# Smaller and reordered transfers, casts and hand-overs at the start of a fused attention and MLP kernel

## The chip, the cores and the metric

The kernel runs on one core of one Trainium2 chip. The metric is device time in microseconds (us), as the median of several executions. The median before is 295.24 us (three runs, 294.39 to 295.44).

## The reference

The first stage is a linear ("efficient") attention over 8 batches, 8 heads, 576 positions and 64 dimensions; the second is an MLP with a leaky ReLU on the 4608 resulting tokens.

```python
q_s = softmax(q, axis=-1)                       # over the 64 dimensions
k_s = softmax(k, axis=2)                        # over the 576 positions
kv  = einsum('bhsd,bhse->bhde', k_s, v)
att = einsum('bhsd,bhde->bhse', q_s, kv)
x   = att.transpose(0, 2, 1, 3).reshape(4608, 512)
h   = x @ w_in                                  # 512 x 2048
out = maximum(0.01 * h, h) @ w_out              # 2048 x 512
```

Inputs and output are float32; the kernel's matmuls take bf16.

## The kernel before, in words

The order of all work is written out by hand: every engine executes its instructions in the order in which the program lists them, and semaphores only make it wait. There is no scheduler.

**Layout.** A batch's q, k and v are loaded as `[128 partitions, 4 head pairs' columns, R = 9 rows, 64]` float32 (`load`, L72, on SyncE's queue, SP). Partitions 0 to 63 hold the even half of the heads and 64 to 127 the other half, and position is split into L = 64 partitions by R = 9 rows. `xT` holds the attention's result transposed, `[128 channels, 4 channel blocks, 4608 tokens]`, in bf16. `w_in_sb` and `w_out_sb` hold the weights in bf16; both are loaded on GpSimd's queue (POOL), which casts from float32 in the transfer. A transfer of w_in covers 64 partitions, two blocks and a range of columns, so one range of columns takes four transfers (`load_w_in`, L129).

**Per batch.** k: a maximum over positions (`k_tree`, `k_allmax`; for batch 0 through TensorE, `k_max_pe` and `k_all_pe`), subtraction (`k_sub`, for batch 0 `k_sub_ps`), `k_exp`. v: a cast to bf16 (`v_cast`, L209), on ScalarE for batches 0 and 1 and on GpSimd later. `kv` (for batch 0 `kv_pair`) multiplies ke by v, with a column of ones for the sum; `kd_make` (or `kd_rec`, `kd_one`) divides by it. q: `q_max`, `q_sub`, `q_exp`, `q_sum`, `q_norm`; for the first four rows of batch 0, `q_first` does the first steps on ScalarE. Then q is turned: batch 0 by TensorE (`q_transpose`, then `q_keep` copies PSUM into `qT`), later batches by a DMA transpose (`q_turn` into `qX`). `attend` or `attend_x` multiplies by kd and copies the result into `xT`.

**The MLP.** It works on 9 tiles of 512 tokens. In `layer1` each of 16 column blocks j of w_in takes four matmuls, one for each channel block, in the order 0, 2, 1, 3; `leaky` on ScalarE copies the PSUM result to a `gj` tile. In `layer2` the 16 blocks of gj are multiplied by w_out, for four groups of 128 tokens; `store` copies the result out of PSUM and issues two DMAs on SP.

**The first tile** is special. It has only batch 0's tokens, and it starts before all of q is there: rows 0 to 3 (RA) give its first 256 tokens. Four pairs of column blocks are begun with the channel blocks 0 and 2 (L641 to L645), then `attend(0, [1, 3], ...)` delivers the other two (L646), and the pairs are finished. `wake` keeps TensorE at work with products of zeros while there is nothing else. The rest of q (R1 is rows 4 and 5, R2 rows 6 to 8) and all of batch 1's preparation hang on hooks: `at(t, u, fn)` puts a step behind unit u of tile t. In tile 0 units 0 to 15 are the column blocks of the first 256 tokens, 16 to 31 those of the second 256, and 32 to 47 the blocks of layer 2.

**Loads.** `gate` is a tiny GpSimd copy that makes POOL's queue wait for some of k before weights are issued; `hold_sync` is a tiny DMA that makes SP's queue wait for a part of a weight before further loads are issued. In the kernel before, SP waits for part of w_in's second half (L560) and then issues k, q and v of batch 1; POOL waits for k of batch 1 (L564) and then issues w_out in five parts. PSUM is handed out in buffers of one bank, six in the pool `psB`.

Of the kernel before, what the change touches and what calls it, by code (L numbers as in the profile page):

```python
# [25 lines left out]
def kernel(  # L26
# [89 lines left out]
    xT = xT_pool.tile([P, NB, T], BF16)  # L116

# [11 lines left out]
    def load_w_in(fh):  # L129
        fs = slice(fh * (F // 2), (fh + 1) * (F // 2))  # L130
        for gg in range(2):
            for hp in range(2):
                nc.gpsimd.dma_start(  # L133
                    out=w_in_t[hp * D : (hp + 1) * D, gg, :, fs], in_=w_in_r[gg, hp, :, :, fs]
                )
# [82 lines left out]
    def q_begin(b):  # L218
        st[b]["qe"] = qe_pool.tile([P, R, HL, D], BF16, name="qe")
        if b == 0:  # L220
            st[b]["qT"] = qT_pool.tile([P, NB, R, L], BF16, name="qT", tag="qT")
# [179 lines left out]
    def q_keep(eng, b, r0, n, gs=slice(0, 4)):  # L401
        o, i = st[b]["qT"][:, gs, r0 : r0 + n], st[b]["ps", r0][:, gs]
        if eng is nc.scalar:
            eng.copy(out=o, in_=i)
        else:
            eng.tensor_copy(out=o, in_=i)

    def attend(b, gs, c0, n, eng):

        ps = psB_pool.tile([P, len(gs), n], FP32, name="po", tag=BANK_TAG)  # L410
        for i, g in enumerate(gs):
            nc.tensor.matmul(
                ps[:, i],
                lhsT=kd2[b % 2][:, g],
                rhs=st[b]["qT"][:, g].rearrange("c r l -> c (r l)")[:, c0 : c0 + n],
                start=True,
                stop=True,
            )
        step = gs[-1] - gs[0] if len(gs) == 2 else 1
        o = xT[:, gs[0] : gs[-1] + 1 : step, b * S + c0 : b * S + c0 + n]  # L420
        if eng is nc.scalar:
            eng.copy(out=o, in_=ps)
        else:
            eng.tensor_copy(out=o, in_=ps)  # L424
# [10 lines left out]
    def attend_x(b, g, rs, eng):  # L435
        hh, gg = divmod(g, 2)
        n = (rs.stop - rs.start) * L
        ps = psB_pool.tile([P, n], FP32, name="po", tag=BANK_TAG)
        qX = st[b]["qX"].rearrange("c (r g) (h l) -> c g h r l", g=2, h=2)
        nc.tensor.matmul(  # L440
            ps.rearrange("p (r l) -> p r l", l=L), lhsT=kd2[b % 2][:, g], rhs=qX[:, gg, hh, rs]
        )
        c0 = b * S + rs.start * L
        o = xT[:, g, c0 : c0 + n]
        if eng is nc.scalar:
            eng.copy(out=o, in_=ps)  # L446
        else:
            eng.tensor_copy(out=o, in_=ps)

    def layer1(j, ph, c0, n, part=slice(0, 4), first=True, last=True):  # L450
        for i, cb in list(enumerate((0, 2, 1, 3)))[part]:
# [3 lines left out]
                rhs=xT[:, cb, c0 : c0 + n],  # L455
# [45 lines left out]
    held = const_pool.tile([1, 2, 128], BF16)  # L501

# [7 lines left out]
    load_w_in(0)  # L510
# [20 lines left out]
    v_cast(nc.scalar, 0, 0)  # L531
    v_cast(nc.scalar, 0, 1)
    k_sub_ps(0, 1)
    nc.gpsimd.tensor_copy(out=gate[:, 0:1], in_=st[0]["k"][:, HL - 1, R - 1, D - 1 : D])
    load_w_in(1)
# [10 lines left out]
    q_keep(nc.scalar, 0, 0, 4, slice(0, 4, 2))  # L546
    q_keep(nc.vector, 0, 0, 4, slice(1, 4, 2))
# [15 lines left out]
    st[1]["v"] = load(v, 1, "v_raw", [(ALLH, ALLR)])  # L563
    nc.gpsimd.tensor_copy(out=gate[:, 0:1], in_=st[1]["k"][:, 0, 0, 0:1])  # L564
    for j0, j1 in ((0, 2), (2, 4), (4, 8), (8, 12), (12, 16)):
        load_w_out(slice(j0, j1))

# [3 lines left out]
    at(0, 11, lambda: q_transpose(0, 4, 2), lambda: q_keep(nc.vector, 0, 4, 2))  # L571
    at(0, 13, lambda: q_transpose(0, 6, 3), lambda: q_keep(nc.vector, 0, 6, 3))
    at(0, 15, lambda: attend(0, [0, 2], 256, 256, nc.scalar))
    at(0, 15, lambda: attend(0, [1, 3], 256, 256, nc.vector))
    at(0, 17, lambda: attend(0, [0, 1, 2, 3], 512, 64, nc.scalar))
    at(0, 15, lambda: k_begin(1), lambda: q_begin(1), lambda: k_tree(1, H0), lambda: k_tree(1, H1))
    at(0, 15, lambda: k_allmax(1), lambda: k_sub(nc.gpsimd, 1, H0), lambda: k_sub(nc.vector, 1, H1))
    at(0, 15, lambda: q_max(1, RA), lambda: q_sub(nc.gpsimd, 1, RA))
    at(0, 15, lambda: q_max(1, RB), lambda: q_sub(nc.gpsimd, 1, RB))
    at(0, 29, lambda: k_exp(1, H1))  # L580
    at(0, 31, lambda: k_exp(1, H0), lambda: v_cast(nc.scalar, 1, 0))
    at(0, 33, lambda: q_exp(1, RA), lambda: q_sum(1, RA), lambda: q_norm(1, RA))
    at(0, 33, lambda: v_cast(nc.scalar, 1, 1), lambda: q_exp(1, RB))
    at(0, 38, lambda: kv(1), lambda: q_sum(1, RB), lambda: q_norm(1, RB), lambda: kd_make(1))
    at(0, 41, lambda: q_turn(1, RA))
    at(0, 43, lambda: q_turn(1, RB))
    at(0, 44, lambda: hold_sync(1, w_out_sb[0:1, 11, 0:128]), lambda: load_all(2))
    for i in range(8):
        at(0, 47, lambda i=i: attend_x(1, i % 4, (RA, RB)[i // 4], nc.scalar))


    XR = (slice(0, 5), slice(5, R))
# [53 lines left out]
    attend(0, [1, 3], 0, 256, nc.scalar)  # L646
# [11 lines left out]
    for j in range(NF):  # L658
        for tsub in range(NTS):
            layer2(pout[tsub], g_sb, tsub, j)  # L660
        if j == NF - 1:
            for tsub in range(NTS):
                store(tsub * P, pout[tsub])
        run(0, 32 + j)
# [57 lines left out]
```

## Time and profile before

| | before |
|---|---|
| median of three runs | 295.24 us |
| the profiled execution, its own time | 293.87 us |
| span of its profile | 292.1 us |
| TensorE (PE) busy | 277.7 us, 95% |
| VectorE (DVE) busy | 145.5 us, 50% |
| ScalarE (ACT) busy | 148.5 us, 51% |
| GpSimd (POOL) busy | 86.0 us, 29% |
| granted TensorE clock | 1.0 |

Times within the profile are counted from the start of the span. "PEld" is TensorE's weight load, which runs beside the matmuls. The page cuts the span into 40 slices and gives each engine's busy tenths. The chain of waits follows the work that ended last backwards, from each step to what released it; in a line of it stand the start, the length and the engine with the line of the kernel. A line of a timeline has the start, the length, the engine, the line, the operation, output and input, and in brackets the idle time before it and what ended that. A DMA's landing time is counted from its issue. The bandwidth that is shown counts bytes as written, so a transfer that casts float32 to bf16 reads twice what is counted.

### The profile page before, as it was taken

The page shows a single profiled execution, that of the slowest core. Times are in us where ns is not written, and L with a number is a line of the kernel's source. Part 1 is how long each engine was busy: PE and PEld are TensorE (multiplying, and loading weights), DVE is VectorE, ACT ScalarE, POOL GpSimd, SP SyncE. Part 2 cuts the span into 40 slices and gives each one's busy share as a digit, 9 for nine tenths or more (in the row PEclk, how much of TensorE's full clock was granted, in tenths as well). Part 3 has the DMA queues.
Part 4 walks back from the last instruction along what each step waited for, and adds up shares of the span by engine and source line. Part 5 has one row for each costly group of instructions (what it writes and reads, how often), then busy time and mean ns, then how long its engine had stood idle before and what let it go on. Part 6 is the DMA issues. An engine that isn't in the chain of part 4 may idle for free.

```text
span 292.1 us, 4216 instructions
## 1 busy us (share of the span) xinstructions
PE 277.7 (95%) x1616; PEld 138.1 (47%) x1643; DVE 145.5 (50%) x240; ACT 148.5 (51%) x268; POOL 86.0 (29%) x61
## 2 busy tenths in 40 slices
PE   6696999999999999999999999999999999999995
PEld 2265844444544455454445444544454444444443
DVE  3947957696790696189276546745540200110011
ACT  4956680678068506941684339533953066016400
POOL 4645280008039208703920391029200000000000
PEclk9999999999999999999999999999999999999999
DMA  7999984989939454963298139913141310131032
GB/s 256 311 212 388 249 134 81 346 302 393 210 75 346 158 117 104 359 187 84 70 336 252 38 72 317 283 39 72 38 81 36 74 36 1 36 79 31 0 73 73
DMA packets 38948, 46.35 MB, mean 159 GB/s; under 512 B 18320, under 2 KB 21648, under 8 KB 38928
## 3 DMA queue, kind: packets, MB, share of 16 engines
q1 hardware_dynamic: 35488, 41.75, 48.7%
q0 software_dynamic: 3280, 4.20, 8.2%
q8 instruction: 13, 0.21, 0.3%
q10 hardware_dynamic: 160, 0.13, 0.1%
q14 instruction: 7, 0.06, 0.1%
HBM read 36.70 MB, written 9.44 MB: 158 GB/s over the span
## 4 chain that ended last, share of the span: by engine, by line
PE 84%; DMA 5%; POOL 3%; DVE 2%; ACT 2%; issue 2%; SPq 0%; POOLq 0%; ACTq 0%
PE pout L473 40%; PE ph L452 39%; DMA w_in_sb<-in_moe_w_in_dram 3%; PE pkv L295 3%; PE po L440 2%; DMA k_raw<-in_k_dram 2%; POOL w_in_sb L133 1%; POOL k_raw L195 1%; DVE t L162 1%; ACT xT L446 1%; ACT vb L213 1%; ACT qe L264 0%; SPq L79 0%; DVE xT L424 0%; DVE m L179 0%
## 5 line engine op out<-in xcount | busy, mean ns | idle before, releaser
L452 PE MATMUL ph<-xT,w_in_sb 128*128 128x512 bf16 (+1 forms) x625 | 126.9, 357 | 4.5 <-DMA w_in_sb<-in_moe_w_in_dram 1.9
L473 PE MATMUL pout<-w_out_sb,gj 128*128 128x512 bf16 (+2 forms) x581 | 128.7, 373 | 0.8 <-issue 0.5
L461 ACT ACTIVATE gj<-ph 128x512 bf16<-128x512 f32 x144 | 82.5, 603 | 58.5 <-PE ph L452 57.9
L452 PEld LDWEIGHTS <-w_in_sb 128*128 128x128 bf16 x640 | 62.1, 98 | 66.2 <-issue 5.4
L473 PEld LDWEIGHTS <-gj 128*128 128x128 bf16 x592 | 57.0, 98 | 62.5
L467 DVE COPY out_sb<-pout 128x512 f32<-128x512 f32 (+1 forms) x34 | 22.7, 675 | 88.2 <-PE pout L473 82.0
L195 POOL TENSOR_TENSOR k_raw<-k_raw,kall 128x2304 f32<-128x2304 f32 (+1 forms) x6 | 29.1, 4842 | 83.6 <-DVE kall L187 69.3
L446 ACT CAST xT<-po 128x256 bf16<-128x256 f32 (+1 forms) x56 | 19.3, 407 | 47.5 <-PE po L440 47.5
L273 DVE TENSOR_REDUCE qsum<-qe 128x36 f32<-128x2304 bf16 (+4 forms) x11 | 19.8, 1799 | 37.8 <-ACT qe L264 37.8
L256 POOL TENSOR_TENSOR q_raw<-q_raw,qmax 128x2304 f32<-128x2304 f32 (+4 forms) x11 | 31.1, 2836 | 25.2 <-DVE qmax L226 25.2
L203 ACT ACTIVATE ke<-k_raw 128x2304 bf16<-128x2304 f32 (+2 forms) x11 | 17.6, 1596 | 10.6 <-POOL k_raw L195 9.4
L280 DVE TENSOR_TENSOR qe<-qe,qrec 128x2304 bf16<-128x2304 bf16 (+4 forms) x12 | 21.7, 1810 | 0.4
L226 DVE TENSOR_REDUCE qmax<-q_raw 128x36 f32<-128x2304 f32 (+4 forms) x11 | 19.4, 1789 | 0.0
L264 ACT ACTIVATE qe<-q_raw 128x2304 bf16<-128x2304 f32 (+4 forms) x11 | 16.9, 1533 | 0.0
L215 POOL CAST vb<-v_raw 128x1152 bf16<-128x1152 f32 x12 | 13.4, 1148 | 0.0
L440 PE MATMUL po<-qX,kd 128*128 128x256 bf16 (+1 forms) x56 | 11.5, 286 | 0.2
L162 DVE TENSOR_TENSOR t<-k_raw 128x1024 f32<-128x1024 f32 (+1 forms) x10 | 10.1, 1011 | 3.1 <-DMA k_raw<-in_k_dram 2.9
L324 PE MATMUL pout<-zero 128*128 128x512 bf16 x26 | 8.8, 466 | 1.4 <-POOL zero L101 1.3
L467 ACT COPY out_sb<-pout 128x512 f32<-128x512 f32 (+1 forms) x3 | 1.6, 549 | 16.5 <-PE pout L473 16.5
L162 DVE TENSOR_TENSOR t<-t 128x256 f32<-128x256 f32 (+2 forms) x20 | 9.6, 478 | 0.7
L295 PEld LDWEIGHTS <-ke 64*128 64x128 bf16 x252 | 7.2, 93 | 3.2 <-ACT gj L461 1.7
L295 PE MATMUL pkv<-vb,ke 64*128 64x129 bf16 x252 | 8.5, 216 | 0.1
(55 smaller groups left out, 94.0 us busy)
## 6 DMA issues: line engine op xcount, KB each, us to landing
out_dram<-out_sb SPq DMA_DIRECT2D x70, 128.0 KB, 2.4
q_raw<-in_q_dram SPq DMA_DIRECT2D x7, 1152.0 KB, 8.7
v_raw<-in_v_dram SPq DMA_DIRECT2D x7, 1152.0 KB, 11.7
k_raw<-in_k_dram SPq DMA_DIRECT2D x6, 1152.0 KB, 5.8
k_raw<-in_k_dram SPq DMA_DIRECT2D x4, 576.0 KB, 5.7
w_in_sb<-in_moe_w_in_dram POOLq DMA_DIRECT2D x8, 256.0 KB, 6.8
w_out_sb<-in_moe_w_out_dram POOLq DMA_DIRECT2D x3, 512.0 KB, 12.0
v_raw<-in_v_dram SPq DMA_DIRECT2D x2, 576.0 KB, 7.3
```

The lines of the kernel that those rows point to most:

```text
L162: nc.vector.tensor_tensor(out=o, in0=i0, in1=i1, op=ALU.max)
L195: eng.tensor_tensor(out=ks, in0=ks, in1=st[b]["kall"][:, hs].unsqueeze(2).to_broadcast([P, n, R, D]), op=ALU.subtract,)
L226: nc.vector.tensor_reduce(out=m, in_=st[b]["q"][:, :, rs], axis=AX.X, op=ALU.max)
L256: eng.tensor_tensor(out=qs, in0=qs, in1=st[b]["qmax", rs.start].unsqueeze(3).to_broadcast([P, HL, n, D]), op=ALU.subtract,)
L273: nc.vector.reduce_sum(out=qsum, in_=st[b]["qe"][:, rs], axis=AX.X)
L280: nc.vector.tensor_tensor(out=qes, in0=qes, in1=st[b]["qrec", rs.start].unsqueeze(3).to_broadcast([P, n, HL, D]), op=ALU.mult,)
L295: nc.tensor.matmul(pkv[hh][:, gg, 0:129], lhsT=st[b]["ke"][rows, r, 2 * gg : 2 * gg + 2].rearrange("p h d -> p (h d)"), rhs=vb2[b % 2][row ...
L446: eng.copy(out=o, in_=ps)
L452: nc.tensor.matmul(ph, lhsT=w_in_sb[:, cb, j * P : (j + 1) * P], rhs=xT[:, cb, c0 : c0 + n], start=(i == 0 and first), stop=(i == NB - 1 a ...
L461: nc.scalar.activation(out=o, in_=ph, func=AF.Prelu, alpha=LEAKY_SLOPE)
L467: copy(out=out_sb, in_=pout)
L473: nc.tensor.matmul(pout, lhsT=g_sb[j // 2][:, j % 2, tsub * P : (tsub + 1) * P], rhs=w_out_sb[:, j, os], start=(j == 0), stop=(j == NF - 1),)
```

## The change

It has five parts.

1. `load_w_in` takes a range of column blocks. The first half of w_in is loaded as before; the second half is issued as two quarters of four transfers each, behind a gate that reads head pair 1 of k and not head pair 3.
2. The first half of batch 0's v is cast by GpSimd, between w_in's first half and the gate.
3. The channel blocks of `xT` are stored in the order 0, 2, 1, 3 (`XB`), and `qT` has a dimension for the head pair, so that blocks 0 and 2 lie side by side. Head groups [0, 2] and [1, 3] are then contiguous. In the first tile, `attend(0, [1, 3], ...)` is listed after the second of the four begun pairs and not after the fourth. The hooks of batch 0's remaining q move from units 11, 13, 15 to 9, 12, 14.
4. Batch 1: q is split into rows 0 to 4 and 5 to 8 (`XR`); its maximum and subtraction go first, the subtraction of k is done by VectorE alone, and the order of ScalarE's work is q_exp, both k_exp, both v casts, q_exp. `kv` moves from unit 38 to 40. Of its eight `attend_x`, the sixth and the eighth are evacuated by VectorE, and the eight stand ahead of the first tile's stores.
5. Batch 1's v is issued on SP's queue only once the first part of w_out has landed; `load_all(2)` follows the second `q_turn` directly.

The diff, in its core:

```diff
@@ w_in @@
-    def load_w_in(fh):
-        fs = slice(fh * (F // 2), (fh + 1) * (F // 2))
+    def load_w_in(j0, j1):
+        fs = slice(j0 * P, j1 * P)
...
-    load_w_in(0)
+    load_w_in(0, 8)
+    v_cast(nc.gpsimd, 0, 0)
     k_begin(0)
...
     k_exp(0, slice(1, 2))
-    v_cast(nc.scalar, 0, 0)
     v_cast(nc.scalar, 0, 1)
+    nc.gpsimd.tensor_copy(out=gate[:, 0:1], in_=st[0]["k"][:, 1, R - 1, D - 1 : D])
+    load_w_in(8, 12)
+    load_w_in(12, 16)
     k_sub_ps(0, 1)
-    nc.gpsimd.tensor_copy(out=gate[:, 0:1], in_=st[0]["k"][:, HL - 1, R - 1, D - 1 : D])
-    load_w_in(1)
     k_exp(0, H1)
@@ layouts @@
+    XB = (0, 2, 1, 3)
...
-            st[b]["qT"] = qT_pool.tile([P, NB, R, L], BF16, name="qT", tag="qT")
+            st[b]["qT"] = qT_pool.tile([P, 2, 2, R, L], BF16, name="qT", tag="qT")
...
-    def q_keep(eng, b, r0, n, gs=slice(0, 4)):
-        o, i = st[b]["qT"][:, gs, r0 : r0 + n], st[b]["ps", r0][:, gs]
+    def q_keep(eng, b, r0, n, ggs=slice(0, 2)):
+        o = st[b]["qT"][:, ggs, :, r0 : r0 + n].rearrange("p g h r l -> p g h (r l)")
+        i = st[b]["ps", r0].rearrange("p (h g) r l -> p g h (r l)", g=2)[:, ggs]
...
-                rhs=st[b]["qT"][:, g].rearrange("c r l -> c (r l)")[:, c0 : c0 + n],
+                rhs=st[b]["qT"][:, g % 2, g // 2].rearrange("c r l -> c (r l)")[:, c0 : c0 + n],
...
-        step = gs[-1] - gs[0] if len(gs) == 2 else 1
-        o = xT[:, gs[0] : gs[-1] + 1 : step, b * S + c0 : b * S + c0 + n]
+        x0 = XB[gs[0]]
+        o = xT[:, x0 : x0 + len(gs), b * S + c0 : b * S + c0 + n]
...
-        o = xT[:, g, c0 : c0 + n]
+        o = xT[:, XB[g], c0 : c0 + n]
...
-                rhs=xT[:, cb, c0 : c0 + n],
+                rhs=xT[:, XB[cb], c0 : c0 + n],
@@ loads of batch 1 @@
     st[1]["q"] = load(q, 1, "q_raw", [(ALLH, ALLR)])
-    st[1]["v"] = load(v, 1, "v_raw", [(ALLH, ALLR)])
     nc.gpsimd.tensor_copy(out=gate[:, 0:1], in_=st[1]["k"][:, 0, 0, 0:1])
     for j0, j1 in ((0, 2), (2, 4), (4, 8), (8, 12), (12, 16)):
         load_w_out(slice(j0, j1))
+    hold_sync(1, w_out_sb[0:1, 1, 0:128])
+    st[1]["v"] = load(v, 1, "v_raw", [(ALLH, ALLR)])
@@ hooks @@
-    at(0, 11, lambda: q_transpose(0, 4, 2), lambda: q_keep(nc.vector, 0, 4, 2))
-    at(0, 13, lambda: q_transpose(0, 6, 3), lambda: q_keep(nc.vector, 0, 6, 3))
-    at(0, 15, lambda: attend(0, [0, 2], 256, 256, nc.scalar))
-    at(0, 15, lambda: attend(0, [1, 3], 256, 256, nc.vector))
-    at(0, 17, lambda: attend(0, [0, 1, 2, 3], 512, 64, nc.scalar))
+    at(0, 9, lambda: q_transpose(0, 4, 2), lambda: q_keep(nc.vector, 0, 4, 2))
+    at(0, 12, lambda: q_transpose(0, 6, 3), lambda: q_keep(nc.vector, 0, 6, 3))
+    at(0, 14, lambda: attend(0, [0, 2], 256, 256, nc.scalar))
+    at(0, 14, lambda: attend(0, [1, 3], 256, 256, nc.vector))
+    at(0, 17, lambda: attend(0, [0, 2, 1, 3], 512, 64, nc.scalar))
     at(0, 15, lambda: k_begin(1), lambda: q_begin(1), lambda: k_tree(1, H0), lambda: k_tree(1, H1))
-    at(0, 15, lambda: k_allmax(1), lambda: k_sub(nc.gpsimd, 1, H0), lambda: k_sub(nc.vector, 1, H1))
-    at(0, 15, lambda: q_max(1, RA), lambda: q_sub(nc.gpsimd, 1, RA))
-    at(0, 15, lambda: q_max(1, RB), lambda: q_sub(nc.gpsimd, 1, RB))
-    at(0, 29, lambda: k_exp(1, H1))
-    at(0, 31, lambda: k_exp(1, H0), lambda: v_cast(nc.scalar, 1, 0))
-    at(0, 33, lambda: q_exp(1, RA), lambda: q_sum(1, RA), lambda: q_norm(1, RA))
-    at(0, 33, lambda: v_cast(nc.scalar, 1, 1), lambda: q_exp(1, RB))
-    at(0, 38, lambda: kv(1), lambda: q_sum(1, RB), lambda: q_norm(1, RB), lambda: kd_make(1))
-    at(0, 41, lambda: q_turn(1, RA))
-    at(0, 43, lambda: q_turn(1, RB))
-    at(0, 44, lambda: hold_sync(1, w_out_sb[0:1, 11, 0:128]), lambda: load_all(2))
+    at(0, 15, lambda: q_max(1, XR[0]), lambda: q_sub(nc.gpsimd, 1, XR[0]), lambda: k_allmax(1))
+    at(0, 15, lambda: k_sub(nc.vector, 1, H0), lambda: k_sub(nc.vector, 1, H1))
+    at(0, 15, lambda: q_max(1, XR[1]), lambda: q_sub(nc.gpsimd, 1, XR[1]))
+    at(0, 32, lambda: q_exp(1, XR[0]), lambda: k_exp(1, H0), lambda: k_exp(1, H1))
+    at(0, 32, lambda: v_cast(nc.scalar, 1, 0), lambda: v_cast(nc.scalar, 1, 1), lambda: q_exp(1, XR[1]))
+    at(0, 32, lambda: q_sum(1, XR[0]), lambda: q_norm(1, XR[0]), lambda: q_turn(1, XR[0]))
+    at(0, 40, lambda: kv(1), lambda: q_sum(1, XR[1]), lambda: q_norm(1, XR[1]), lambda: kd_make(1))
+    at(0, 43, lambda: q_turn(1, XR[1]), lambda: load_all(2))
     for i in range(8):
-        at(0, 47, lambda i=i: attend_x(1, i % 4, (RA, RB)[i // 4], nc.scalar))
+        eng = nc.vector if i in (5, 7) else nc.scalar
+        at(0, 47, lambda i=i, eng=eng: attend_x(1, i % 4, XR[i // 4], eng))
@@ first tile @@
         begun.append(ph)
-    attend(0, [1, 3], 0, 256, nc.scalar)
+        if j == 2:
+            attend(0, [1, 3], 0, 256, nc.scalar)
...
             layer2(pout[tsub], g_sb, tsub, j)
+        run(0, 32 + j)
         if j == NF - 1:
             for tsub in range(NTS):
                 store(tsub * P, pout[tsub])
-        run(0, 32 + j)
```

More of the change, by code (lines that the diff above doesn't have):

```diff
@@ L501 @@
     held = const_pool.tile([1, 2, 128], BF16)
+    XR = (slice(0, 5), slice(5, R))
     def hold_sync(i, src):
@@ L545 @@
         kd_one(nc.vector, 0, 0, hh)
-    q_keep(nc.scalar, 0, 0, 4, slice(0, 4, 2))
-    q_keep(nc.vector, 0, 0, 4, slice(1, 4, 2))
+    q_keep(nc.scalar, 0, 0, 4, slice(0, 1))
+    q_keep(nc.vector, 0, 0, 4, slice(1, 2))
     attend(0, [0, 2], 0, 256, nc.scalar)
@@ L588 @@
     for i in range(8):
-        at(0, 47, lambda i=i: attend_x(1, i % 4, (RA, RB)[i // 4], nc.scalar))
-    XR = (slice(0, 5), slice(5, R))
+        eng = nc.vector if i in (5, 7) else nc.scalar
+        at(0, 47, lambda i=i, eng=eng: attend_x(1, i % 4, XR[i // 4], eng))
     for b in range(3, B):
```

## The prediction

> **What bounds the kernel now.** I read the page first. PE is busy 95% of the span. Its row over 40 slices of 7.3 us:
>
> ```profile
> PE   6696999999999999999999999999999999999995
> ```
>
> The low digits stand in the first four slices; later it is at 9 tenths to the last. So time is won early, and whatever starts the second token tile earlier moves the whole tail. Next I read the chain of waits, in order of time (start us, us, what). Its early pieces:
>
> ```profile
> 7.96 2.50 POOL w_in_sb L133 x4
> 10.46 2.23 issue
> 12.70 0.02 POOLq L256
> 12.71 0.19 POOL gate L534
> 12.90 1.67 POOL w_in_sb L133 x3
> 14.57 9.07 DMA w_in_sb<-in_moe_w_in_dram
> 23.64 0.14 issue
> 23.77 1.69 PE ph L452 x14
> ...
> 51.69 2.20 ACT xT L446 x7
> 53.88 0.04 issue
> 53.93 1.24 PE ph L452 x5
> ```
>
> The reader sees the last of w_in's transfers holding PE until 23.77, and after that the evacuations of batch 1's attention holding the second tile until 53.93. Third, the waits of PE alone, from 14 to 56 us (total, times, longest):
>
> ```profile
> PE ph L452 <- DMA w_in_sb<-in_moe_w_in_dram: 1.9, 1, 1.9
> PE ph L452 <- ACT xT L422: 1.4, 2, 0.7
> ```
>
> The 1.4 are two stops, 19.12 to 19.79 and 28.21 to 28.93 in PE's timeline. Fourth, VectorE's timeline, since a wait that goes lets the next one show. It carries the rest of batch 0's q (rows R1 and R2):
>
> ```profile
> 22.06 0.69 DVE L273 TENSOR_REDUCE qsum<-qe 128x8 f32<-128x512 bf16 x1 [3.54 <-ACT qe L264]
> 22.78 0.20 DVE L275 RECIPROCAL qrec<-qsum 128x8 f32<-128x8 f32 x1
> 23.02 0.69 DVE L280 TENSOR_TENSOR qe<-qe,qrec 128x512 bf16<-128x512 bf16 x1
> 23.63 0.95 DVE L273 TENSOR_REDUCE qsum<-qe 128x12 f32<-128x768 bf16 x1
> 24.61 0.23 DVE L275 RECIPROCAL qrec<-qsum 128x12 f32<-128x12 f32 x1
> 24.87 0.96 DVE L280 TENSOR_TENSOR qe<-qe,qrec 128x768 bf16<-128x768 bf16 x1
> ```
>
> R2's q is normalised at 25.83, R1's at 23.71. PE turns them at 26.39 and 25.30, so this chain ends only 0.5 us ahead of PE.
>
> **Step 1, half of v on GpSimd.** ACT gives up one cast of 1152 elements (two of them take 2.19, so 1.1). On POOL the same shape takes 1137 to 1158 ns in all twelve of its runs. It starts behind the four first w_in issues at 10.46 (that v landed at 2.29 + 6.8 = 9.1) and ends near 11.6; its ke is ready at 12.07, so kv_pair(0,0) starts near 12.1 and not at 13.16. The full 1.06 does not arrive: q_transpose waits for q_norm, which VectorE ends at 14.07, while before it started at 14.66 behind wake(4). So q_transpose, kv_pair(0,1), the copy of qT, attend and its evacuation move by 0.53 to 0.57, and the first layer1 matmul goes from 17.00 to 16.43. Queued behind the cast on POOL are the gate and w_in's second half; the gate now waits for the subtraction ending at 11.36 and not the one at 12.65, so w_in issues from 11.9 rather than 12.83.
>
> **Step 2, head pairs.** q_keep on VectorE still follows ScalarE's (the changed instruction list keeps that wait), so qT's new order is worth nothing. attend([1,3]) goes ahead of two of the four begun pairs: it runs at 17.3 (kd ready at 16.6), is evacuated by 18.2, and PE passes from the begun pairs to their second halves at 18.43 without the 0.67 stop, against 19.79 before. Gain so far 1.36.
>
> **Step 3, w_in in quarters.** It adds four issues at 0.6 us on POOL, and the last four wait for the first half's landings (13.7, 14.8, 16.3, 17.4), so POOL is done at 18.0 instead of 15.2; next in its queue is q_sub of R1, which began at 17.74 and now begins at 18.0. Its reader, q_exp, comes at 20.04, so 0.3 us is hidden by a margin of 1 us. The transfers are bound by bandwidth: DMA share is over 1.0 in every 2 us window from 4 to 40 us, and the three 256 KB parts of the second half landed 1.2 to 1.3 us apart (18.7, 20.0, 21.2). Quarters of 128 KB then land 0.63 apart, the third quarter at 20.0, the fourth at 22.5. The fourth is earlier than 23.64 because batch 1's k, held until part of the last columns is there, now goes out at 21.3 and not at 19.39. PE reaches column block 8 at 18.43 + 16 matmuls x 0.109 = 20.2. The 1.85 stop is gone.
>
> The Trainium skill ("DMA: Bandwidth & Descriptors", Anatomy of one DMA) gives each software DMA about 2 us of fixed cost beside its bytes, and its rules for kernel authors want 1 MiB or more in one, which speaks against quarters. If that cost were paid in series, the four extra DMAs would add 8 us by an estimate from that page. The rows above, 256 KB every 1.25 us with several in flight, do not show it paid in series.
>
> **Step 4, what is late next.** The q chain. q_exp R1 stands behind two leakys on ScalarE and so moves with step 2 by 1.36: R1 is normalised at 22.35, R2 at 24.47. But the transposes were moved up, to units 9 and 12. PE is at unit 9's hook at 21.07 and waits 1.3 us; from 22.35 it turns R1 (0.25), does blocks 10 to 12 (1.3), waits from 23.9 to 24.47, turns R2 (0.5), does 13 and 14 (0.86), four attends (0.5) and 15 (0.43), and stands at 26.75. ScalarE's evacuation (0.58) ends then; VectorE's (0.69) ends at 27.05, 0.1 us late. Before, the second half of the tile could start at 28.93. Gain 2.1: of the 1.85 and 0.72 stops won, some 1.9 comes back as a wait for q.
>
> **Step 5, layer 2.** The second half needs 7.1 us as before, so layer 2 starts at 33.95 and not 36.03. w_out must hold against that. Batch 1's k lands at 25.3 (24.9 before), q at 29.7 (29.4). In the windows from 24 to 30 us 392 to 407 GB/s move, that is the fp32 loads almost alone; from 32 us 202 to 215, w_out alone, counted at half its reads. So w_out gets through when q is done: its first part at about 30.9 (33.3 before, behind v), the second at 32.2, needed at 33.95 and 35.7. v goes out at 31.5. Batch 2's k, as large and alone, took 6.0 us to land, so v lands near 38. Meanwhile w_out's third part (j 4 to 7) is pushed to about 37.6 against a need of 37.4. I take 0.1, with 0 to 0.9 as bounds.
>
> **Step 6, batch 1.** VectorE starts k at 26.95 (28.85 before). Its work grows by one subtraction (1.36) that POOL gave up: 3.6 trees, 1.5 q_max, 2.3 k_allmax, 2.7 subtractions, 1.2 q_max, to 38.3. ScalarE: q_exp 34.4 to 35.7, k_exps to 38.3, v casts (2.3) to 40.6, q_exp to 41.7. kv now stands behind block 8, at 33.95 + 9 x 0.862 = 41.7. It is ready with 1 us to spare. q_turn of the second part follows at 44.4 and lands at 47.8 (3.4 us, as before); attend_x is due at 49.3. Nothing waits there.
>
> **Step 7, attend_x.** ScalarE had eight evacuations in 2.52; now it has six and VectorE two, in parallel. That is worth about 0.3 of the 2.20 in the chain, bounds 0 and 0.65. The four output copies on VectorE now follow them (2.48 us), with batch 2's trees behind, at 53.7 and not 56.07, shifted as much as PE. Batch 2's loads go out some 4 us earlier. So the tail shifts as a whole.
>
> **Sum.** 2.1 + 0.3 - 0.1 (w_out) - 0.1 (rounding of late hand-overs) = 2.2 us. The profiled execution took 293.87 (span 292.1 and 1.8 around it), so it would be 291.7. The median of the runs shown is 295.24, 1.4 above that execution; it becomes 293.0.
>
> **Rivals.** First, the gain is mostly eaten: the early shift of 0.55 fails (VectorE is held up while POOL casts; its norm took 2.12 at 71.10 beside POOL's casts against 1.49 at 46.42), and w_out's third part costs its full 0.9. Against it: the VectorE subtractions beside this cast read PSUM and fp32, and one beside POOL at 34.82 took 1.36 against 1.32. It gives 2.2 - 0.55 - 0.8, so 0.8 us: 294.4.
>
> Second, slower: v, sent behind w_out's first part, is late. Its price begins when v lands later than 39.4, since two casts (2.25) stand between it and kv at 41.7. If v is only served after all the software queue's work, the DMA engines have 2.5 MB of w_out reads and 1.18 MB of v left at 33.6; at 410 GB/s v lands at 42.6 to 42.8. kv then waits 3.4 us, and 2.2 - 3.4 makes it 1.2 slower: 296.4. From a landing at 41.6 on the change loses. For it: v is last in line. Against it: from 28 to 30 us, with w_out issued at 25.8, 392 GB/s still moved, so plain loads went ahead of w_out.
>
> The Trainium skill ("DMA: Bandwidth & Descriptors", Queues, rings and completion order) has the engines take turns between queues by packet. By an estimate from that page v and w_out would share evenly and v land at 39.4, at the edge where it starts to cost. The window just named shows no even turns.
>
> Third, the q chain costs nothing because it starts earlier than I think (ScalarE's first leakys come at once): then PE loses only the evacuation at the half's end, and the second half starts at 25.4 and not 28.93. With step 7 and the 0.2 of losses that is 3.6: 291.6.
>
> **How the numbers follow.** Forecast 0.55, first rival 0.22, second 0.13, third 0.10. A measurement here can tell about 0.5%, 1.5 us, from no change. The forecast case (1.4 to 2.9 us) and the third lie beyond it nearly always: faster 0.64. The first rival and the second at its lower prices: same 0.24. The second with another delay on top: slower 0.12. Range 291.3 to 296.0: the third rival with step 7 at its upper bound, and most of the second rival's way to 296.4.
>
> **What would show it.** Right: the first layer1 matmul near 16.4; no wait of PE for w_in; waits of PE for VectorE's qe before two transposes, some 1.3 and 0.5 us; layer 2 from 34; kv from 41.7 without a wait; the second tile from 51.5. Wrong: a wait of PE for w_out or of ScalarE for v of over 1 us, or layer 2 starting at 35 or later.

## The result, and the profile after

The changed kernel takes 297.34 us (median of nine runs, 296.20 to 299.83), the kernel before 295.19 us in the same comparison. The ratio is 1.0094 with a 95% interval of 1.0071 to 1.0118: slower by 2 to 3 us, where 2.2 us were to be won. The profiled execution took 299.2 us (span 297.4), so it lies 1.9 above its median, while that of before (293.87) lies 1.3 below; of the 5.3 us between the two spans some 3 are the choice of execution. Part of the difference among executions goes with a clock: most executions of before have a mean granted TensorE clock of 0.994 (21 of the 31 of one comparison), the profiled one 1.0; those of the changed kernel have 0.977 to 0.988.

The rows of the page over 40 slices (7.4 us each) show where it differs. First PE, then its granted clock:

```profile
PE   6597996999999999999999999999999999999995
PEclk9779998999999999999999999999999999999999
```

The clock was 9 in every slice before. It is now low in the second and third slice and again in the seventh, and the low busy digit in that slice (6) is new as well. From the ninth slice on the two pages are alike: the second token tile starts at 58.99 instead of 53.27 (there with a stop of 0.28 right behind its first matmuls, here with none), so 5.4 later in effect, and the span is 5.3 longer. So all of it happens in the first 59 us.

The chain of waits of the changed kernel (start us, us, what):

```profile
9.64 0.66 DVE t L163
10.30 0.59 POOL w_in_sb L134
10.89 1.16 POOL vb L216
...
16.64 5.20 DMA w_in_sb<-in_moe_w_in_dram
...
22.53 4.65 DMA k_raw<-in_k_dram
...
28.24 5.46 DMA w_out_sb<-in_moe_w_out_dram
...
34.27 12.05 DMA v_raw<-in_v_dram
...
46.35 2.22 ACT vb L214 x2
...
57.25 1.42 ACT xT L448 x4
```

Before, the chain went over w_in to PE at 23.77. Now it never touches PE before 48.6: it runs from GpSimd's cast (`vb` on POOL) through w_in, batch 1's k, w_out's first part and v to the casts of v, each load issued only when the one before had landed. (Between the cast and the gate it has 1.80 us as "issue"; the gate reads head pair 1 of k, whose subtraction on VectorE ended at 13.72.) The waits of PE from 8 to 62 us (total, times, longest):

```profile
PE kT L331 <- POOL gate L512: 2.3, 1, 2.3
PE pkv L296 <- ACT vb L214: 2.1, 2, 1.7
PE kT L331 <- DVE kmax L163: 2.0, 1, 2.0
PE psum_qt L390 <- ACT gj L463: 1.3, 1, 1.3
PE psum_qt L390 <- DVE qe L281: 0.4, 1, 0.4
```

The waits for w_in (1.9) and for `xT` (1.4) are gone, and the two before q's transposes are there as forecast. (The first of them carries ScalarE's name, but the leaky had long been done; VectorE's norm of R1, ending at 26.13, is what came last.) The first row lies in front of the first k maximum and was 1.7 before. The second and third were not forecast, and the experiments will show them to be the two causes.

**The first, near 11 us.** VectorE's timeline of the changed kernel, at the last steps of k's maximum for the second half:

```profile
9.19 1.69 DVE L163 TENSOR_TENSOR t<-t 128x256 f32<-128x256 f32 x2
10.91 1.28 DVE L163 TENSOR_TENSOR kmax<-t,k_raw 128x128 f32<-128x128 f32 x1
```

POOL's timeline at the same time:

```profile
10.85 1.19 POOL L216 CAST vb<-v_raw 128x1152 bf16<-128x1152 f32 x1
```

The same steps in the kernel before:

```profile
8.76 0.74 DVE L162 TENSOR_TENSOR t<-t 128x256 f32<-128x256 f32 x2
9.54 0.29 DVE L162 TENSOR_TENSOR kmax<-t,k_raw 128x128 f32<-128x128 f32 x1
```

A step of 0.29 us takes 1.28 when it lies beside GpSimd's cast, and the one ahead of it is stretched by 0.95 too. The maximum is ready at 12.19 instead of 9.83 (0.43 of that is a later first load), PE waits 1.95 us for it, and its clock is half from 11.6 to 18.4: kv_pair takes 1.16 instead of 0.68. The first layer1 matmul comes at 20.25, before at 17.00.

**The second, near 46 us.** ScalarE's wait from 8 to 62 us:

```profile
ACT vb L214 <- DMA v_raw<-in_v_dram: 4.3, 1, 4.3
```

v is issued at 34.27 and lands at 46.35. kv starts at 47.55 (42.16 before) after 1.75 us of standstill, waits 0.37 more for the second cast, and then PE has half clock again from 49.1 to 52.5: layer 2's 27 matmuls behind kv take 7.39 us, against 5.99 for the same ones at full clock in the run with v early below.

### The profile page after: what moved, and what is told of

The parts are those of the page before. It is cut to its first block, busy times and chain, and to the rows that moved or that the text cites. A ratio compares the mean times of both kernels' runs of the same rounds, so it can differ in the third digit from the quotient of the medians.

```text
span 297.4 us, 4224 instructions
## 1 busy us (share of the span) xinstructions
PE 281.5 (95%) x1616; PEld 139.7 (47%) x1643; DVE 149.5 (50%) x243; ACT 146.8 (49%) x265; POOL 86.0 (29%) x65
## 2 busy tenths in 40 slices
DMA packets 39524, 46.35 MB, mean 156 GB/s; under 512 B 18384, under 2 KB 22736, under 8 KB 39504
## 4 chain that ended last, share of the span: by engine, by line
PE 81%; DMA 11%; POOL 2%; ACT 2%; issue 2%; DVE 1%; SPq 1%; ACTq 0%; POOLq 0%
PE pout L475 39%; PE ph L454 37%; DMA v_raw<-in_v_dram 4%; DMA k_raw<-in_k_dram 3%; PE pkv L296 3%; PE po L442 2%; DMA w_out_sb<-in_moe_w_out_dram 2%; DMA w_in_sb<-in_moe_w_in_dram 2%; DVE t L163 1%; POOL w_in_sb L134 1%; ACT vb L214 1%; ACT xT L448 1%; POOL vb L216 0%; SPq L507 0%; POOL gate L567 0%
## 5 line engine op out<-in xcount | busy, mean ns | idle before, releaser
L196 POOL TENSOR_TENSOR k_raw<-k_raw,kall 128x2304 f32<-128x2304 f32 x5 | 25.3, 5066 | 77.8 <-DVE kall L188 63.6
L448 ACT CAST xT<-po 128x320 bf16<-128x320 f32 (+1 forms) x54 | 18.8, 405 | 47.7 <-PE po L442 47.7
L204 ACT ACTIVATE ke<-k_raw 128x2304 bf16<-128x2304 f32 (+2 forms) x11 | 17.5, 1596 | 11.7 <-POOL k_raw L196 8.6
L227 DVE TENSOR_REDUCE qmax<-q_raw 128x36 f32<-128x2304 f32 (+4 forms) x11 | 19.5, 1788 | 0.0
L216 POOL CAST vb<-v_raw 128x1152 bf16<-128x1152 f32 x13 | 14.6, 1151 | 0.0
L442 PE MATMUL po<-qX,kd 128*128 128x320 bf16 (+1 forms) x56 | 11.6, 286 | 0.3
L325 PE MATMUL pout<-zero 128*128 128x512 bf16 x26 | 10.0, 513 | 1.5 <-POOL zero L101 1.3
L163 DVE TENSOR_TENSOR t<-t 128x256 f32<-128x256 f32 (+2 forms) x20 | 10.5, 526 | 0.7
## 6 DMA issues: line engine op xcount, KB each, us to landing
v_raw<-in_v_dram SPq DMA_DIRECT2D x7, 1152.0 KB, 11.6
```

The lines of the kernel that those rows point to most:

```text
L163: nc.vector.tensor_tensor(out=o, in0=i0, in1=i1, op=ALU.max)
L196: eng.tensor_tensor(out=ks, in0=ks, in1=st[b]["kall"][:, hs].unsqueeze(2).to_broadcast([P, n, R, D]), op=ALU.subtract,)
L227: nc.vector.tensor_reduce(out=m, in_=st[b]["q"][:, :, rs], axis=AX.X, op=ALU.max)
```

## The experiments

The theory: two parts of the change each cost more than the other three win. GpSimd's cast holds up VectorE's two-input steps in SBUF, and v behind w_out's first part comes too late; both leave PE standing, and the clock then makes it dearer. The rivals: one of the two does it all; the head pairs, quarters and the new order of batch 1 are themselves at fault; or the clock alone is. Ratios below are against the kernel before, run on the same chip beside them, with 95% intervals.

### Undo one part, the other, both

**Cast back on ScalarE** (the changed kernel otherwise):

```diff
     load_w_in(0, 8)
-    v_cast(nc.gpsimd, 0, 0)
...
+    v_cast(nc.scalar, 0, 0)
     v_cast(nc.scalar, 0, 1)
```

> The changed kernel with the first half of batch 0's v cast by ScalarE again, everything else as changed. Theory 1 (the GpSimd cast holds VectorE's k_tree beside it: the second k maximum ended at 12.19 us instead of 9.83, PE then stood still for 2 us and its granted clock fell to 0.5 until 18.8): the k_tree steps of the second half take 0.29 to 0.43 us each again, the clock stays 1.0 from 10 to 20 us, and the first layer1 matmul starts at 17.0 to 17.5 instead of 20.25. Rival (the late prologue comes from slower first loads or from the quarters of w_in): the first layer1 matmul stays near 20. Theory 2 (v of batch 1 is late, it landed at 46.3): that wait stays or grows, kv starts near 45 to 46 and the time falls by only 1 to 2 us, to 295.5 to 296.5.

Measured: 296.36 us, ratio 1.0047 (1.0024 to 1.0070). The two steps of k's maximum take 0.74 and 0.29 again, and the first layer1 matmul comes at 18.60. It is not 17.0, as kv_pair now waits 1.44 us for ScalarE's cast, as it did before, and half clock follows for 3.4 us. v still lands late (44.9), kv waits 1.95 and 0.37. Still slower: the cast is not all of it.

**v ahead of w_out again** (the changed kernel otherwise):

```diff
     st[1]["q"] = load(q, 1, "q_raw", [(ALLH, ALLR)])
+    st[1]["v"] = load(v, 1, "v_raw", [(ALLH, ALLR)])
...
-    hold_sync(1, w_out_sb[0:1, 1, 0:128])
-    st[1]["v"] = load(v, 1, "v_raw", [(ALLH, ALLR)])
```

> The changed kernel with batch 1's v loaded directly behind its q again, ahead of w_out. Theory 2: the wait of ScalarE's v cast (4.3 us) and of PE's kv (1.75 + 0.37 us) goes, and the clock stays 1.0 from 49 to 53 us, where it was 0.5; that is worth 2.4 us of waiting and about 1.7 us of slow clock, some 4 us: 293 to 294. The first layer1 matmul stays near 20.2. Rival (w_out then lands later and PE waits for it instead): PE waits for w_out from 36 to 38 us, and the time stays at 296 to 298.

Measured: 294.80 us, ratio 1.0000 (0.9975 to 1.0025). kv runs at 45.38 without a wait, and from 20 us on the clock is full. The stretched steps and the 1.95 us wait are as in the changed kernel. So v's place makes 0.94% of it, 2.8 us. The time is above the 293 to 294 expected, and level with the kernel before: the cast alone eats about what the other parts win, not more.

**Both undone:**

```diff
-    v_cast(nc.gpsimd, 0, 0)
...
+    v_cast(nc.scalar, 0, 0)
...
+    st[1]["v"] = load(v, 1, "v_raw", [(ALLH, ALLR)])
...
-    hold_sync(1, w_out_sb[0:1, 1, 0:128])
-    st[1]["v"] = load(v, 1, "v_raw", [(ALLH, ALLR)])
```

> Both undone: v's cast on ScalarE, batch 1's v ahead of w_out; w_in in quarters, the head-pair order, the earlier hooks and batch 1's new order stay. If the two theories are all that made the change slower, the steps that are left give the forecast's rest: first layer1 matmul near 17, layer 2 from 34 to 34.5, 2 us faster than before: 293 to 293.5. If there is a third cause (the order of batch 1, w_out's landing), it is 294.5 or more, with a new wait of PE that the profile names.

Measured: 293.48 us, ratio 0.9966 (0.9943 to 0.9989): faster than before by 1.0 us. That is half of the 2 us expected, and layer 2 starts at 36.34 and not at 34 to 34.5, as the first layer1 matmul comes at 18.72, behind a stretch of half clock. Taken together, the head pairs, the quarters and batch 1's order win; that they are at fault as a whole is ruled out, and what each is worth, the quarters apart (below), was not separated. Set on top of this kernel, the cast costs 0.34% (1.0 us, about what the intervals of the two ratios allow as noise; 0.47% where v is late too, 0.53% on the kernel before), v's place 0.81% (2.4 us; 0.94% with the cast), and the two together 1.28%, 3.8 us.

### Each of the two alone, on the kernel before

**Only the cast:**

```diff
     load_w_in(0)
+    v_cast(nc.gpsimd, 0, 0)
...
-    v_cast(nc.scalar, 0, 0)
```

> The kernel before with one edit: the first half of batch 0's v cast by GpSimd behind w_in's first half, as in the change. Theory 1 (the cast holds VectorE's operations that read two SBUF inputs, whatever else was changed): the two t steps and the k maximum of the second head pairs take about 3 us instead of 1.03, the second k maximum ends near 12 instead of 9.83, the clock falls to 0.5 for two stretches (run mean 0.988 and not 0.994 to 1.0), and the first layer1 matmul comes near 19.5 to 20. Since PE later waits less for w_in, the time is 1 to 2.5 us above before. Rival (the cast does harm only with the quarters and the moved gate): the k maximum ends near 9.9 and the time is within 0.5 us of before or below.

Measured: 296.13 us, ratio 1.0053 (1.0030 to 1.0075). VectorE's and POOL's timelines of this run:

```profile
8.78 1.68 DVE L162 TENSOR_TENSOR t<-t 128x256 f32<-128x256 f32 x2
10.49 1.29 DVE L162 TENSOR_TENSOR kmax<-t,k_raw 128x128 f32<-128x128 f32 x1
```

```profile
10.44 1.19 POOL L215 CAST vb<-v_raw 128x1152 bf16<-128x1152 f32 x1
```

Nothing else was changed, and the same two steps are stretched by the same 1.94 us; PE's wait for `kmax` is 1.95. The first layer1 matmul comes at 18.96 (17.00 before), somewhat earlier than the 19.5 to 20 expected, behind one window of half clock in this profile and not two. The step at 10.49 lies wholly beside the cast and lasts 0.1 longer than it. But the step ahead, two instructions that would have ended at 9.52, ends at 10.46, so its hold begins by 9.5 at the latest, 0.9 before the cast's recorded start. Why so early stays open (a record on POOL is rough).

**Only v's place:**

```diff
-    st[1]["v"] = load(v, 1, "v_raw", [(ALLH, ALLR)])
...
+    hold_sync(1, w_out_sb[0:1, 1, 0:128])
+    st[1]["v"] = load(v, 1, "v_raw", [(ALLH, ALLR)])
...
-    at(0, 44, lambda: hold_sync(1, w_out_sb[0:1, 11, 0:128]), lambda: load_all(2))
+    at(0, 44, lambda: load_all(2))
```

> The kernel before with one edit: batch 1's v issued only once w_out's first part has landed (and SP's later wait on w_out gone with it). Theory 2: v is issued near 30 to 32, lands 11 to 12 us later, at 42 to 44, ScalarE's v cast waits for it, kv starts 2 to 4 us late and PE's clock falls to 0.5 for 3 to 4 us behind it: 3 to 5 us above before. Rival (v is late only because the changed kernel loads w_in later): v lands by 39 to 40 and the time is within 1 us of before.

Measured: 297.06 us, ratio 1.0098 (1.0058 to 1.0137). PE's timeline where kv stands:

```profile
44.09 0.69 PE L295 MATMUL pkv<-vb,ke 64*128 64x129 bf16 x18 [0.80 <-ACT vb L213]
46.09 0.69 PE L295 MATMUL pkv<-vb,ke 64*128 64x129 bf16 x18 [1.31 <-ACT vb L213]
```

v was issued at 31.41 and landed 11.45 later, at 42.86. Here it went out as early as the prediction had it, so the late landing is not a consequence of the cast. In one thing the expectation failed: the clock didn't fall behind kv here. The wait fell into two windows of the clock's grid (last section) with 2.61 and 2.10 us of PE in them, and 1.0 was granted in both and after. So v's late landing costs its wait even without the clock. Both parts are slower by themselves, each without the other.

### The clock by itself

**v early, with the hole filled** (v ahead of w_out as above; zeros for PE while it waits for `kmax`):

```diff
     k_all_pe(0, 0)
-    wake(2)
+    wake(12)
```

> The kernel with v early (its cast on GpSimd stays) with ten more matmuls of zeros behind the first k_all_pe, where PE stands still for 2 us. They are 2.1 us of PE work in a hole of 1.95. If the slow clock from 11 to 19 us follows from PE's standing still there, the clock stays 1.0, the first layer1 matmul comes at 18.5 to 19 instead of 20.25, and the time is 1 to 1.5 us below the kernel with v early. If the clock does not depend on that hole, the clock is 0.5 there all the same and the time is equal or up to 0.3 us more.

Measured: 294.28 us, ratio 0.9995 (0.9965 to 1.0026). The clock is full throughout the profile, the VectorE steps are stretched as before, and the first layer1 matmul comes at 18.47 instead of 19.75: the clock had cost 1.28 us there. In the total only some 0.5 of it shows (294.80 to 294.28), within the intervals and short of the 1 to 1.5 expected, as layer 2 now comes early enough to wait 0.84 us for w_out. The clock alone is not the cause either: with all of it granted the start is still 1.47 later than 17.00.

**Both undone, with the hole behind kv_pair's wait filled:**

```diff
     k_all_pe(0, 1)
-    wake(2)
+    wake(8)
```

> Both edits undone as in e3_both, with six more matmuls of zeros behind the second k_all_pe, in the 1.44 us in which PE stands still for v's cast. Theory 3 (the slow stretch of e3_both, 0.83 granted from 10 to 20 us, follows from that standstill): the clock is 1.0 throughout in nearly every run, the first layer1 matmul comes at 17.0 instead of 18.72, and the time is 0.5 to 1.5 us below e3_both: 292 to 293. If the standstill isn't the cause, clock and time are those of e3_both.

Measured: 293.60 us, ratio 0.9958 (0.9936 to 0.9980). The first layer1 matmul is at 17.17 (18.72 without the zeros), layer 2 at 34.79 (36.34), and then 0.70 us go to w_out's third part. Against both parts undone (0.9966) that is no measurable step: the next wait takes it.

### What of VectorE the cast holds

**The cast behind the second gate,** beside the subtraction that reads PSUM; the rest as in the kernel with the lowest median (next section):

```diff
-    v_cast(nc.scalar, 0, 0)
     v_cast(nc.scalar, 0, 1)
...
+    v_cast(nc.gpsimd, 0, 0)
     load_w_in(8, 12)
     load_w_in(12, 16)
```

> e8_wout_first with the first v cast on GpSimd again, but behind the second gate, where VectorE runs the third subtraction (1152 elements, one input from PSUM; 1.3 us before) and then a reciprocal and q_norm. Theory 1 in its narrow form (the cast holds only operations with two inputs from SBUF): the subtraction keeps its 1.3 to 1.4 us beside the cast, and nothing on VectorE is over 0.3 us longer than in e8_wout_first, unless q_norm (1.22) starts before the cast ends. Rival (the cast holds every VectorE operation): the subtraction takes 2 us or more.

One execution, 293.54 us. VectorE and POOL:

```profile
11.84 1.35 DVE L357 TENSOR_TENSOR k_raw<-k_raw,kallp 128x1152 f32<-128x1152 f32 x1 [0.19 <-issue]
```

```profile
11.89 1.15 POOL L216 CAST vb<-v_raw 128x1152 bf16<-128x1152 f32 x1
```

The subtraction (`kallp` is in PSUM) runs beside the whole cast and takes 1.35 us, as in every other profile. It is not held, and neither is the cast, at 1.15 (1.14 to 1.16 in the kernel before), though it began second. The maximum's steps, both of whose inputs are in SBUF, are.

**A memset in the cast's place,** of as many elements of an unused tile, with the cast on ScalarE:

```diff
     load_w_in(0, 8)
+    nc.gpsimd.memset(junk, 0.0)
```

> e8_wout_first with a GpSimd memset of 1152 bf16 elements of an unused tile where the change had the cast (both v casts stay on ScalarE): GpSimd only writes, about 1.1 us. If it is GpSimd's reading that holds VectorE, the t steps and the k maximum of the second head pairs keep 0.74 and 0.29 us. If any GpSimd work on SBUF does it, they take 1.7 and 1.3 us as in e5_before_cast.

One execution, 293.91 us:

```profile
9.63 0.29 DVE L163 TENSOR_TENSOR kmax<-t,k_raw 128x128 f32<-128x128 f32 x1
```

```profile
10.51 1.11 POOL L515 MEMSET junk<- 128x1152 bf16 x1
```

Nothing is stretched. The comparison is not a clean one: with these starts the maximum is done (9.92) ahead of the memset. Yet the cast's record in the run with only the cast began no earlier (10.44), and there the steps were held from 9.5 on. So it isn't the four w_in issues ahead of it that hold VectorE; whether a write beside a two-input step would, was not seen.

### Versions that win

**w_out's first part ahead of the gate on k,** on top of both undone and `wake(8)`:

```diff
+    load_w_out(slice(0, 2))
     nc.gpsimd.tensor_copy(out=gate[:, 0:1], in_=st[1]["k"][:, 0, 0, 0:1])
-    for j0, j1 in ((0, 2), (2, 4), (4, 8), (8, 12), (12, 16)):
+    for j0, j1 in ((2, 4), (4, 8), (8, 12), (12, 16)):
```

> As e7_both_wake, with w_out's first part issued ahead of the gate on batch 1's k, so that it follows w_in directly. Theory: layer 2 begins without a wait for w_out (it would wait 0.7 to 1 us in e7_both_wake, where the first part lands near 35), batch 1's k lands about 1 us later but VectorE takes it up only at 27 to 28: 0.5 to 1 us below e7_both_wake. If the later k holds VectorE, batch 1's kv waits and nothing is won.

Measured: 292.96 us (seven runs, 292.62 to 293.05), ratio 0.9944 (0.9924 to 0.9964). It has the lowest median here, and is 0.56% faster than before; from the kernel without this edit (0.9958) the ratio can't tell it, so the 0.5 to 1 us expected didn't show. The first layer1 matmul is at 17.00, layer 2 at 34.62, the second tile at 52.90. What is late next, from 8 to 62 us:

```profile
PE pout L475 <- DMA w_out_sb<-in_moe_w_out_dram: 1.0, 1, 1.0
```

**w_out's second part ahead of it too:**

```diff
     load_w_out(slice(0, 2))
+    load_w_out(slice(2, 4))
```

> e8_wout_first with w_out's second part, too, ahead of the gate. The wait of PE for w_out's third part (1.0 us at 39.2 in e8_wout_first) goes, as 0.5 MB of reads leave the queue ahead of it; batch 1's k lands about 1.2 us later, at 30 to 30.5, for which kv has 2 us of margin: 0.5 to 1 us below e8_wout_first, 292 to 292.5. If k comes too late after all, ScalarE's v casts end behind PE's arrival at kv and the time is that of e8_wout_first or more.

Measured: 293.47 us, ratio 0.9939 (0.9910 to 0.9968), no better. The wait for the third part is 1.46 now: batch 1's k lands later behind more weights, and the gate behind it runs at 29.31 (26.37 with one part ahead), with all that follows.

**w_in's second half whole,** in four transfers as before (otherwise the kernel with w_out's first part ahead):

```diff
-    load_w_in(8, 12)
-    load_w_in(12, 16)
+    load_w_in(8, 16)
```

> e8_wout_first with w_in's second half in four transfers again instead of eight. If the quarters matter as the forecast had it (block 8's columns there at 20 and not at 22.5): PE reaches block 8 at 20 and waits some 2 us for w_in, of which the wait for q (1.28 and 0.42) hides most: 0.3 to 1 us slower than e8_wout_first. Rival (the q chain hides it all, or fewer transfers land earlier): no difference.

Measured: 293.85 us, ratio 0.9947 (0.9916 to 0.9978), the same as with quarters. PE's first row of waits:

```profile
PE ph L454 <- DMA w_in_sb<-in_moe_w_in_dram: 2.7, 1, 2.7
```

PE stands 2.65 us for w_in at 23.90, and in turn no longer for q (1.28 and 0.42 with quarters) nor for w_out (1.0): 2.65 against 2.70. The quarters' gain is handed on whole to the waits behind it.

## Why the prediction was wrong, by its own steps

**Step 1 failed.** It had the first layer1 matmul at 16.43, 0.57 earlier; it came at 20.25, 3.25 later. The cast's own length (1.14 to 1.16 predicted, 1.19 measured) and its place behind the four issues (10.46 predicted, 10.85) were right. Wrong was which of VectorE's work lies beside it: the step took k's maximum to be over by then (it ended at 9.83 in the profile before) and weighed only the subtractions, which are indeed not held. The hold begins about 0.9 us ahead of the cast's record and takes in the last steps of the maximum. The pieces, from the runs: the hold is worth 1.47 at the first layer1 matmul (18.47 with the hole filled, against 17.00), the clock 1.28, and the rest is a first load of k that came later in this execution. The first rival had named the mechanism ("VectorE is held up while POOL casts") and then set two rows against it. The subtractions beside this cast read PSUM, a kind that is spared. The other row, the subtraction at 34.82, has both its inputs in SBUF (`kall` is not in PSUM). VectorE's and POOL's timelines of the kernel before:

```profile
34.82 1.36 DVE L195 TENSOR_TENSOR k_raw<-k_raw,kall 128x1152 f32<-128x1152 f32 x1
```

```profile
34.94 3.74 POOL L195 TENSOR_TENSOR k_raw<-k_raw,kall 128x1152 f32<-128x1152 f32 x1 [5.41 <-DVE kall L187]
```

VectorE's began first, and it was GpSimd's that took long: 3.74, where its five of twice the size took 5.06 to 5.07, which makes 2.5 for this one by an estimate. So the row doesn't show that nothing is held; by these records it shows the other engine held. It was the right mechanism, and two witnesses misread.

The Trainium skill speaks against this part in so many words ("SBUF — State Buffer", Who interferes with whom): VectorE's second read and GpSimd share a port, so that an instruction of VectorE with two SBUF inputs contends with one of GpSimd that reads SBUF, one holding the other off whole, while one with a single SBUF input (outside its two-port modes) or a GpSimd write alone does not. The runs agree for the step beside the cast (0.29 to 1.28, the cast's 1.19 and a little) and for the PSUM operand (1.35); for the early begin no run here gives a reason, and a GpSimd write beside a two-input step was not seen. The prediction didn't weigh this rule.

**Steps 2, 3 and 4 held.** No wait for `xT`, none for w_in (nor with PE on time, from 17.00 on, in the kernel with w_out's first part ahead), and waits of 1.28 and 0.43 before the two transposes, 1.3 and 0.5 predicted. From the first layer1 matmul to layer 2 the changed kernel takes 17.6 us, predicted 17.5, before 19.0. Only the start was wrong, so layer 2 stood at 37.87 and not at 33.95. In the runs without cast and clock loss it stood at 34.62 and 34.79, and the prediction's chain from 17.0 on gives 34.5. The run with halves shows the other half of step 4: what q hides is the whole of the quarters' worth.

**Step 5 failed in its transfer.** w_out's first part landed at 33.7 (30.9 predicted), v was issued at 34.27 (31.5): this delay comes down from step 1, as the gate on k and w_in's second issue moved from 11.9 to 14.31. But v then took 12.05 us where 6.5 were reckoned; alone on the kernel before, issued at 31.41, it took 11.45. The price of w_out's third part, 0.1 with 0.9 as bound, can't be read in the changed kernel, as PE came too late to meet it; in the runs with v ahead of w_out, which is another order, and full clock in the profile it was 0.7 to 1.9, and nothing in the run with halves, where PE had waited for w_in.

What the transfer did can be read in the windows of the changed kernel (after the engines' busy times: granted clock, DMA share, GB/s):

```profile
34.00:36.00 2.00, 2.00 (x20) 1.80 (x19) 1.97 (x4) 1.45 (x3) 0.03 (x1) 1.00 1.07 157
36.00:38.00 2.00, 2.00 (x20) 1.77 (x19) 1.82 (x8) 1.24 (x3) 2.00 (x1) 1.00 1.23 202
38.00:40.00 2.00, 1.95 (x10) 0.88 (x9) 1.90 (x3) 1.93 (x3) 0.29 (x1) 1.00 1.17 275
40.00:42.00 2.00, 2.00 (x11) 0.91 (x10) 2.00 (x3) 2.00 (x2) 0.00 (x0) 1.00 1.13 299
```

Until 38 us only w_out moves (up to some 200 GB/s counted, half its reads), though v was issued at 34.27. The trace's packets, split by queue, say the same: no byte of v before 38.2, 3.9 us after its issue (3.8 in the run with only v's place), then 187 to 217 GB/s of v beside 82 to 95 of w_out from 39 to 44, and 2 us more, with a last trickle of packets, to the landing. Put together: 3.9 + 6 + 2 = 12. Before has the mirror image: w_out was issued at 25.8 and its first bytes came at 29.9, 4 us later, while k, q and v moved. That wait for the first bytes is what the prediction read, in the window from 28 to 30, as plain loads going ahead of w_out. The packets show no such order, only a late start of the later queue, and one of no fixed length: in the changed kernel w_out, issued at 28.24 while q moved, had its first bytes at 29.99, 1.8 us later. What sets it, no run here shows. Once both run they share: from 40 to 43 us the packets of w_out hold the engines 52% of the time, those of v 60% (packets of the two overlap). The rule on even turns, which the prediction set aside, describes this part well; the estimate made from it, 39.4, lacked the 3.9 us ahead and the 2.8 of the later issue.

**Step 6 failed with it.** kv was due at 41.7 without a wait and came at 47.55 with one of 1.75, then 0.37. The second rival had this wait, and its place and turning point too (a landing beyond 41.6 loses). Its reason, v served only after all of the software queue's work, is not what the packets show, as the two shared; that its landing of 42.6 to 42.8 agrees with the 42.86 of the run with only v's place is luck. It gave 296.4 and was taken for the unlikelier case by the misread window. The second rival and the first rival's hold of VectorE came at once, where the prediction had priced them one at a time. The second rival's price was short of what the standstill did to the clock in the profile of the changed kernel: one window of half clock, 7.39 against 5.99 for the 27 matmuls. Both signs that the prediction named as proof against it came: a wait of ScalarE for v of over 1 us (4.3), and layer 2 after 35 (37.87).

**Step 7** was sized at 0.3, between 0 and 0.65. From the start of batch 1's attention to the second tile it takes 2.08 us now (56.91 to 58.99) without a stop behind it, and took 1.89 and a stop of 0.28 before (51.38 to 53.27): 0.1 by these records, inside the bounds. **The sum:** with the cast and the new place of v taken out, the other steps win 1.0 us (0.9966), not the forecast's 2.2. Of the 1.2 that are missing 0.57 was step 1's; the other part that shows is the wait for w_out, 0.4 to 1.0 in the two kernels with both undone and in the one with w_out's first part ahead, reckoned at 0.1.

## What to carry to other kernels

Before work is given to an idle engine, list what the other engines do within a microsecond of both its ends, and for each whether its operands come from the same memory; a row that shows no hold counts only for its own kind of operands and its own order of starts, and the other engine's row beside it must be read too. A load put behind another queue's traffic should be priced from a row with that same traffic around it, with its time to the first bytes, not from one that ran alone. And on an engine that bounds the kernel at 95%, a stop of 2 us early on is not priced by its length: look for what it does to the clock, and fill it with idle work if it can't be avoided.

## What the runs showed of the hardware

**The granted clock changes on a fixed grid.** In all fourteen profiles each stretch of half or full clock that is complete lasts a whole number of 3.413 us: two of half clock in the changed kernel (6.83 us), then nine full (30.72), one half, 72 full. Windows laid on that grid show when it drops (PE busy is the second time, the clock the third number from the end). The kernel before, then the run with both parts undone, both with the same 1.44 us wait for ScalarE's cast of v:

```profile
8.54:11.95 3.41, 2.53 (x15) 0.78 (x14) 3.34 (x9) 3.33 (x16) 1.92 (x4) 1.00 1.09 368
11.95:15.37 3.42, 2.13 (x33) 1.44 (x36) 2.94 (x7) 3.35 (x5) 2.49 (x5) 1.00 1.12 204
```

```profile
9.87:13.29 3.42, 1.68 (x9) 0.47 (x8) 3.39 (x7) 3.34 (x11) 2.13 (x6) 1.00 1.11 296
13.29:16.70 3.41, 3.16 (x27) 2.09 (x29) 1.88 (x5) 2.09 (x2) 2.52 (x5) 0.50 1.11 202
```

In the first the grid cuts the wait in two and PE is busy over 2 us in each window; the clock stays full. In the second the wait falls into one window, PE is busy 1.68 us of it, and the next window has half clock. The grid lies differently in each execution, and with it the loss. At full clock, a window with over 1.75 us of PE was followed by another at full clock in every profile up to the second tile, and each drop came behind one with 1.1 to 1.7. It isn't a sharp bound by these records: some windows with 1.4 to 1.7 had no drop behind them, among them 22.09 to 25.50 with 1.60 in the run with halves. The changed kernel's 1.49 (8.14 to 11.56) and 1.30 (45.69 to 49.10) both had one. A window of half clock was followed by a second one only where PE was busy 2.72 us of it (the changed kernel) and 1.91 (the run with v early); after 3.08 and more the clock was full again. The Trainium skill ("TensorE: Matmul & The Clock Gate", What's actually happening) has the window, 3413 ns and free-running, and half clock after an idle one; the runs agree on the window, but a window half idle was enough.

**What it costs.** In the run with w_in in halves the three executions at 1.0 took 292.37 to 292.75 us and the seven at 0.992 or 0.994 had a median of 294.05, 1.4 us more, though one of the seven took 292.58. In the kernel before, of one comparison, four executions at 0.999 or 1.0 had a median of 294.14 and those at 0.993 or 0.994 one of 294.98, 0.8 us more, with times from 293.7 up among both. It need not show in the total: the kernel with w_out's first part ahead took 292.91 and 292.62 at 0.994, as at 1.0; that a later wait hides it there is likely but not shown.
